# Windowed attention and a feed-forward layer: the loads of transposed probabilities of pairs 4 to 7 are issued by ACT instead of SyncE, and the first batch's order is planned anew

## Chip, core and metric

The kernel runs on one core of a Trainium2 chip. The metric is the time of one execution in microseconds (us), measured on the device. Engines are named as in the profile: PE is TensorE (matmuls), DVE is VectorE, ACT is ScalarE, POOL is GpSimd, SP is SyncE, which issues DMAs. PE accumulates in PSUM banks; the other engines but POOL read them.

## What is computed

Attention over 8 batches and 8 heads, with a window of 32 positions to each side and 32 global positions, and then a feed-forward layer with a leaky slope over all 4608 rows:

```python
k_all = concat([k_g, k_l]);  v_all = concat([v_g, v_l])
out_g = softmax(scale * q_g @ k_all.T) @ v_all            # 32 global rows of a head
s_ll  = where(abs(i - j) <= 32, scale * q_l @ k_l.T, -1e9)
s_l   = concat([scale * q_l @ k_g.T, s_ll])
out_l = softmax(s_l) @ v_all                               # 512 local rows of a head
x = concat([out_g, out_l]) as 4608 x 512
h = x @ w_in                                               # 512 x 2048
g = max(h, 0) + alpha * min(h, 0)
out = g @ w_out                                            # 2048 x 512
```

The weights arrive as float64 and are decoded on the chip into an upper and a lower float32r part.

## The kernel before

Two heads of one batch form a pair; a batch has four pairs, 32 in all. A batch of 512 rows goes through 16 blocks f of the feed-forward layer (128 hidden units each). While PE multiplies the blocks of one batch, the attention of the next batch's pairs is woven in between. The first batch is special: pairs 0 to 3 are computed ahead of it, and in it the weights are decoded, block by block, while pairs 4 to 7 are computed. From the second batch on, the decoded weights are in place.

The order of the first batch on every engine is not written by hand. `early` (L153) lists operations with an engine, a cost in us, the operations that they need and, for some, a due time; `Plan.run` (L94) is a list scheduler that picks the next operation by the earliest possible start and then by due time less a bias for its kind, and `begin` issues the instructions in the order found. Each engine then runs its own instructions strictly in that order, and waits in front of an instruction whose inputs are not there. The numbers of the plan stand in `LIST` (L38). The names of operations, as used below (a number behind a name is the pair or the block):

- S: local scores of a pair on PE; red, ex, rza, rzr, nm: its softmax on DVE, ACT and POOL, in tile p.
- G: global scores on PE; gm, gexp, gz, gsc: their softmax on DVE and ACT, in tile sg_sb.
- tq and tr: DVE transposes 32 x 32 squares of p and of sg_sb. sq and sr: four DMAs each scatter them to DRAM (scratch). hq and hr: one DMA each loads them back, fully transposed, into tile pt (512 KB and 192 KB). Pairs 0 to 3 transpose on PE instead (T, Tg).
- V: PE multiplies pt by the values (tile v); the first four matmuls need hq alone, the rest hr too. V of a pair and G of the next write one PSUM tile, and G of the next stands right behind V or one operation later. xA, xB, xg copy the result out.
- Lq, Lv, Lw: SP's loads of q and k, of v, and of raw weights; cv, ab, d1, d2, d3, ia, ca, su: decoding of half a block on ACT, DVE and POOL; wf and wo: SP's stores of decoded weights.
- f1 of a block: 12 matmuls x times w_in (rows h_ps). n, p, gh, gl: slope and split of the result (ACT, DVE, ACT, DVE). fa: 8 matmuls with gh and w_out, fb: 4 matmuls with gl (both are rows o).

There is one p, one v and one pt tile for pairs from 4 on: the next pair's red waits until sq has read p, the next Lv and hq until V is done. Every DMA of the first batch is issued by SP in the planned order. A DMA instruction that waits for its source stops SP, and all behind it. In particular hq waits on SP for the landing of sq, and hr for that of sr; the plan allowed a negative lag of 100 us between two operations of SP, that is, it did not count this wait:

```python
lag = (0.12 if e != "SP" else -100.0) if y == e else 0.3 if y == "PE" else 0.12
```

The helper lines L280 (all engines but PE) and L309 (matmuls) record every instruction, so the profile's line numbers say nothing; tiles and shapes tell the operations apart.

Of the kernel before, what the change touches and what calls it, by code (L numbers as in the profile page):

```python
# [35 lines left out]
GOFF = 1024  # L36
GROWS = {1: (0, 0), 4: (0, 1), 7: (0, 2), 10: (1, 0), 13: (1, 1), 15: (1, 2)}
LIST = dict(  # L38
    first=37.579, pace=5.504, pair0=70.66, pair=20.171, slack=2, vsub=1, ahead=4, inflight=4, near=0.1, vgl=1, half=True,
    bias=dict(tq=-6, V=12, ex=-3, ca=-3, hr=6, gz=0, xB=12, hq=-1, Lw=-7, sr=12, ab=3, gsc=0, Lq=-6, be=5, rzr=1, yh=3, gexp=-12, cv=-1, ia=1, xA=3, red=-3),  # L40
)
FAST = range(2 * NF, NB * NF)
CATCH = (16, 23, 30)
# [15 lines left out]
class Plan:  # L59
# [3 lines left out]
        self.slots = {k: [0.0] * n for k, n in slots.items()}  # L63
        self.ops, self.slack, self.near, self.bias = {}, slack, near, bias

    def op(self, name, engine, cost, needs=(), lock=False, take=(), free=(), kind=None, due=None, n=1):
        assert name not in self.ops, name
        self.ops[name] = dict(engine=engine, cost=cost, needs=[x for x in needs if x], lock=lock, take=take, free=free, kind=kind, due=due, n=n)

    def due_times(self):  # L70
        users = {n: [] for n in self.ops}
# [23 lines left out]
    def run(self):  # L95
        ops, users = self.ops, self.due_times()
        end, order = {}, []
        free = dict(PE=5.4, ACT=2.5, DVE=5.0, POOL=4.0, SP=1.2)
        lock, dma, kind = 0.0, 3.3, None
        left = {n: len(o["needs"]) for n, o in ops.items()}  # L100
        ready = {n for n, k in left.items() if k == 0}
        while ready:
            can = []
            for n in sorted(ready):
                o = ops[n]
                e = o["engine"]
# [12 lines left out]
            assert can, sorted(ready)
            t, _, n = min(can)  # L120
            e = ops[n]["engine"]
            t, _, n = min((c for c in can if ops[c[2]]["engine"] == e and c[0] <= t + self.near), key=lambda c: (c[1], c[0]))
            o = ops[n]
            cost = o["cost"]
            if e == "PE":
                cost = cost * (1.25 if t < 45 else 1.0) + (0.3 if kind != o["kind"] else 0.0)
                kind = o["kind"]
            if e == "SP":
                free[e] = t + 0.48 * o["n"]
                dma = max(dma, t + 1.6) + cost  # L130
# [22 lines left out]
def early(first, pace, pair0, pair, slack, vsub, ahead, inflight, near, vgl=0, half=False, bias={}):  # L153

    plan = Plan({"st": NST - 2, "w": NWB}, slack, near, bias)
    op = plan.op
    for P in range(9):
        pre = P < NRAW
        op(f"Lq{P}", "SP", 1.72, [f"G{P-2}", f"S{P-2}"] if P > 1 else [])
# [4 lines left out]
        due = pair0 + pair * (P - 5) if P > 4 else None  # L164
# [32 lines left out]
        last = first + pace * 15.5 if P == 8 else None  # L197
        if not pre:
            op(f"tq{P}", "DVE", 1.23, [f"nm{P}.0", f"nm{P}.1"], due=last)
            op(f"sq{P}", "SP", 1.31, [f"tq{P}"], n=4, due=last)  # L200
        if P == 8:
            break
        pb = [f"V{P-1}"] if P else []
        if pre:
            op(f"T{P}", "PE", 1.1, [f"nm{P}.0", f"nm{P}.1"] + ([f"pt0{P-1}", f"pt1{P-1}"] if P else []), kind="t", free=(("w", 1),) if P % 2 else ())
            op(f"pt0{P}", "ACT", 0.49, [f"T{P}"] + pb)
            op(f"pt1{P}", "DVE", 0.60, [f"T{P}"] + pb)
            op(f"Tg{P}", "PE", 0.45, [f"gsc{P}", f"T{P}", f"ptg{P-1}" if P else None], kind="t")
            op(f"ptg{P}", "ACT", 0.40, [f"Tg{P}"] + pb)
            lb = [f"pt0{P}", f"pt1{P}", f"ptg{P}"] + ([f"ex{P+1}.0", f"ex{P+1}.1"] if P < 3 else ["xlA1", "xlB1", "xg1"])  # L210
        else:
            op(f"tr{P}", "DVE", 0.5, [f"gsc{P}", "clear"])
            op(f"hq{P}", "SP", 1.31, [f"sq{P}"] + pb)
            op(f"sr{P}", "SP", 0.5, [f"tr{P}"], n=4)
            op(f"hr{P}", "SP", 0.5, [f"sr{P}", f"hq{P}"])
            lb = [f"hq{P}", f"hr{P}", f"mem{P+1}", f"Lq{P+1}"]
        op(f"V{P}", "PE", 2.0, [f"Lv{P}"] + lb, kind="v", free=(("w", 2),) if pre and P % 2 else ())
        if not pre:
# [7 lines left out]
        if not pre:  # L226
            c = P - NPAIR
# [8 lines left out]
    for k in range(2 * NF):  # L236
        f, j = divmod(k, 2)
# [12 lines left out]
    for t in range(NF):  # L250
        x = [f"xl{a}{P}" for P in range(NPAIR) for a in "AB"]
# [37 lines left out]
def longformer_ffn(ctx: ExitStack, tc: tile.TileContext, qk, v, w, alpha, out):  # L289
# [31 lines left out]
    sync = Engine(tc, nc.sync, pin_sync)  # L321
# [561 lines left out]
    def begin():  # L883
# [9 lines left out]
        def issue(name):  # L893
# [297 lines left out]
```

## Time and profile before

| | us |
|---|---|
| median of 3 runs | 928.39 |
| lowest to highest | 928.23 to 931.25 |
| the profiled execution, its own time | 927.88 |
| its span, first to last instruction | 926.1 |

One execution was profiled. In the table of stretches, each row has the stretch, its length, the busy time of each engine with the number of its instructions, the clock that TensorE was granted as a share of full speed, the share of the DMA engines' time that was busy, and GB/s. A row of a timeline has the start, the duration, engine, line, operation, output<-input, the number of merged instructions and, in brackets, the idle time ahead of it and what ended it. A row of waits has the engine, the tile that it was to write, whom it waited for, us in total, how often, and the longest. Rows "SPq" are SP's queue of DMA instructions.

### The profile page before, as it was taken

The page shows a single profiled execution, that of the slowest core. Times are in us where ns is not written, and L with a number is a line of the kernel's source. Part 1 is how long each engine was busy: PE and PEld are TensorE (multiplying, and loading weights), DVE is VectorE, ACT ScalarE, POOL GpSimd, SP SyncE. Part 2 cuts the span into 40 slices and gives each one's busy share as a digit, 9 for nine tenths or more (in the row PEclk, how much of TensorE's full clock was granted, in tenths as well). Part 3 has the DMA queues.
Part 4 walks back from the last instruction along what each step waited for, and adds up shares of the span by engine and source line. Part 5 has one row for each costly group of instructions (what it writes and reads, how often), then busy time and mean ns, then how long its engine had stood idle before and what let it go on. Part 6 is the DMA issues. An engine that isn't in the chain of part 4 may idle for free.

```text
span 926.1 us, 22539 instructions
## 1 busy us (share of the span) xinstructions
PE 885.9 (96%) x8668; PEld 764.9 (83%) x8668; DVE 608.7 (66%) x1676; ACT 388.6 (42%) x1166; POOL 312.7 (34%) x275
## 2 busy tenths in 40 slices
PE   7798968999999999999999999999999999999998
PEld 5676646787888888888888888888888899899898
DVE  5887757877577666866677667766686656544532
ACT  6877655553444433443345333443344322211211
POOL 3444433255444333433223323322343322222221
PEclk7889889799999999999999999999999999999999
DMA  8968977999665866586667667586657552645630
GB/s 306 348 178 322 341 252 271 337 362 358 232 208 177 294 210 197 189 277 217 211 228 253 230 224 225 187 262 217 201 181 269 185 192 91 205 160 180 205 116 24
DMA packets 86811, 211.19 MB, mean 228 GB/s; under 512 B 23985, under 2 KB 44465, under 8 KB 82865
## 3 DMA queue, kind: packets, MB, share of 16 engines
q1 hardware_dynamic: 86704, 209.76, 67.0%
q8 instruction: 68, 1.11, 0.5%
q14 instruction: 39, 0.31, 0.1%
HBM read 165.95 MB, written 43.78 MB: 226 GB/s over the span
## 4 chain that ended last, share of the span: by engine, by line
PE 67%; DMA 13%; DVE 9%; ACT 6%; SPq 2%; issue 2%; POOL 0%; DVEq 0%; ACTq 0%
PE o L309 30%; PE h_ps L309 28%; PE o_ps L309 4%; ACT p L280 3%; DMA scratch<-sg_sb 3%; PE s_ps L309 3%; DMA wraw<-in_w_dram 2%; PE g_ps L309 2%; DVE g L280 2%; DMA scratch<-p 2%; SPq L280 2%; DVE xl L280 2%; DMA pt<-scratch 1%; DMA alpha_sb<-in_alpha_dram 1%; DVE x_raw L280 1%
## 5 line engine op out<-in xcount | busy, mean ns | idle before, releaser
L280 POOL TENSOR_TENSOR gl<-g,gh 128x512 fp32r<-128x512 f32 (+1 forms) x128 | 159.1, 1243 | 375.8 <-ACT gh L280 306.0
L309 PE MATMUL h_ps<-xh,wt 128*128 128x256 f32 (+1 forms) x1120 | 241.0, 309 | 4.1 <-DVE wt L280 3.7
L309 PE MATMUL o<-gh,wo 128*128 128x512 f32 (+1 forms) x1024 | 244.3, 381 | 0.0
L280 ACT CAST gh<-g 128x512 fp32r<-128x512 f32 (+1 forms) x144 | 85.8, 596 | 306.5 <-DVE g L280 304.2
L309 PEld LDWEIGHTS o<-gh,wo 128*128 128x128 f32 x1024 | 176.8, 188 | 31.9 <-issue 0.4
L309 PEld LDWEIGHTS h_ps<-xh,wt 128*128 128x128 f32 x1120 | 182.4, 189 | 24.4 <-issue 6.1
L309 PE MATMUL h_ps<-xl,wt 128*128 128x256 f32 (+1 forms) x560 | 171.6, 306 | 0.8 <-DVE xl L280 0.8
L309 PE MATMUL o<-gl,wo 128*128 128x512 f32 (+1 forms) x512 | 131.1, 378 | 0.0
L280 DVE TENSOR_SCALAR g<-h_ps,alpha_sb 128x512 f32<-128x512 f32 (+1 forms) x128 | 91.5, 715 | 41.1 <-PE h_ps L309 35.4
L309 PEld LDWEIGHTS h_ps<-xl,wt 128*128 128x128 f32 x560 | 105.8, 189 | 6.6 <-DVE xl L280 1.0
L309 PE MATMUL h_ps<-xh,s 128*128 128x256 f32 x576 | 105.4, 279 | 2.9 <-DVE h_ps L280 2.0
L309 PEld LDWEIGHTS o<-gl,wo 128*128 128x128 f32 x512 | 92.8, 188 | 18.4
L280 POOL TENSOR_TENSOR p<-p,rz 128x512 f32<-128x512 f32 x64 | 69.2, 1101 | 101.1 <-DVE rz L280 95.2
L309 PEld LDWEIGHTS h_ps<-xh,s 128*128 128x128 f32 x576 | 90.7, 188 | 8.1 <-issue 4.0
L280 DVE TENSOR_TENSOR h_ps<-u,h_ps 128x256 f32<-128x256 f32 x144 | 61.1, 424 | 49.1 <-PE h_ps L309 47.5
L280 ACT ACTIVATE p<-p,mn 128x128 f32<-128x128 f32 x224 | 86.9, 396 | 4.8 <-DVE mn L280 4.8
L280 DVE SCALAR_TENSOR_TENSOR g<-h_ps,g 128x512 f32<-128x512 f32 (+1 forms) x128 | 84.1, 657 | 4.2
L309 PE MATMUL h_ps<-xl,s 128*128 128x256 f32 x288 | 80.6, 280 | 0.9 <-DVE xl L280 0.7
L280 DVE TENSOR_TENSOR u<-u,h_ps 128x256 f32<-128x256 f32 x96 | 40.3, 420 | 62.1 <-PE h_ps L309 38.7
L280 POOL TENSOR_TENSOR wt<-wt,wr 128x512 int32<-128x512 int32 x32 | 45.8, 1433 | 93.4 <-DVE wt L280 73.4
L309 PE MATMUL o_ps<-pt,v 128*64 128x32 f32 (+1 forms) x1600 | 59.8, 234 | 15.2 <-DMA pt<-scratch 13.2
L309 PEld LDWEIGHTS o_ps<-pt,v 128*64 128x64 f32 x1600 | 55.2, 149 | 22.4 <-DMA pt<-scratch 10.7
(88 smaller groups left out, 1046.1 us busy)
## 6 DMA issues: line engine op xcount, KB each, us to landing
wo<-wo SPq DMA_DIRECT2D x128, 512.0 KB, 4.4
v<-in_v_dram SPq DMA_DIRECT2D x30, 1024.0 KB, 5.8
qk<-in_qk_dram SPq DMA_DIRECT2D x32, 672.0 KB, 7.0
wraw<-in_w_dram SPq DMA_DIRECT2D x32, 512.0 KB, 7.4
scratch<-p SPq DMA_DIRECT2D x112, 128.0 KB, 3.0
pt<-scratch SPq DMA_DIRECT2D x28, 512.0 KB, 5.5
wo<-wt SPq DMA_DIRECT2D x16, 512.0 KB, 8.5
out_dram<-ost SPq DMA_DIRECT2D x32, 256.0 KB, 3.3
```

The source lines that it names most:

```text
L280: ins = op(*a, **k)
L309: ins = nc.tensor.matmul(*a, **k)
```

## The change

The plan may give a DMA to ACT (`move`, with the list `aq`), and `LIST` names hq and hr. On ACT such an operation costs 0.45 us in the plan, starts when what it needs has landed, and lands 2.2 us plus twice its transfer later. The lag of -100 us between two SP operations stays for all but names that begin with h. A DMA is counted 2.0 us from issue to transfer instead of 1.6, and PE's work after 45 us is counted 5% longer. The numbers in `LIST` were searched anew: among them `inflight`, which lets cv run six half blocks ahead of su instead of four, `vgl`, by which gl is split between POOL (even blocks) and DVE (odd blocks) where DVE did all, and the biases of all kinds. `scatter` and `fetch_pt` take the queue as an argument. Code behind the first batch is not changed; pairs from 8 on still load through SP.

```diff
 LIST = dict(
-    first=37.579, pace=5.504, pair0=70.66, pair=20.171, slack=2, vsub=1, ahead=4, inflight=4, near=0.1, vgl=1, half=True,
+    first=37.895, pace=5.449, pair0=70.632, pair=19.178, slack=2, vsub=1, ahead=4, inflight=6, near=0.1, vgl=2, half=True, aq="hq hr",
...
-                    lag = (0.12 if e != "SP" else -100.0) if y == e else 0.3 if y == "PE" else 0.12
+                    lag = -100.0 if y == e == "SP" and n[0] != "h" else 0.3 if y == "PE" else 0.12
...
-                cost = cost * (1.25 if t < 45 else 1.0) + (0.3 if kind != o["kind"] else 0.0)
+                cost = cost * (1.25 if t < 45 else 1.05) + (0.3 if kind != o["kind"] else 0.0)
...
-                dma = max(dma, t + 1.6) + cost
+                dma = max(dma, t + 2.0) + cost
                 stop = dma + 0.8
+            elif o["dma"]:
+                free[e] = t + cost
+                dma = max(dma, t + 2.0) + o["dma"]
+                stop = free[e] + 2.2 + 2 * o["dma"]
...
+    def move(name, dma, needs, n=1, due=None):
+        if name.rstrip("0123456789") in aq:
+            op(name, "ACT", 0.45 * n, needs, dma=dma, due=due)
+        else:
+            op(name, "SP", dma, needs, n=n, due=due)
...
-            op(f"hq{P}", "SP", 1.31, [f"sq{P}"] + pb)
-            op(f"sr{P}", "SP", 0.5, [f"tr{P}"], n=4)
-            op(f"hr{P}", "SP", 0.5, [f"sr{P}", f"hq{P}"])
+            move(f"hq{P}", 1.31, [f"sq{P}"] + pb)
+            move(f"sr{P}", 0.5, [f"tr{P}"], 4)
+            move(f"hr{P}", 0.5, [f"sr{P}", f"hq{P}"])
...
-    def fetch_pt(P, x):
+    def fetch_pt(P, x, queue=sync):
         sc = scratch.pop((P, x)).rearrange("j k c n -> (j k) (c n)")
         o, n = ((0, 1024), (GOFF, 384))[x]
-        sync.dma_start(new_pt(P)[:, o : o + n], sc)
+        queue.dma_start(new_pt(P)[:, o : o + n], sc)
...
-                {"t": transpose_dve, "s": scatter, "h": fetch_pt}[k[0]](n, "qr".index(k[1]))
+                if k[0] == "t":
+                    transpose_dve(n, "qr".index(k[1]))
+                else:
+                    {"s": scatter, "h": fetch_pt}[k[0]](n, "qr".index(k[1]), act if plan.ops[name]["engine"] == "ACT" else sync)
```

The instructions' order, engine by engine, moves in the first batch. SP's rows for pair 5 before, from wo2 over sq5, wf6, hq5, a weight load and sr5 to hr5:

```order
L280 DMA wo<-wt 128x1024
L280 DMA scratch<-p 32x4x256 x4
L280 DMA wf<-wt 128x512
L280 DMA pt<-scratch 128x1024
L280 DMA wraw<-in_w_dram 128x1024
L280 DMA scratch<-sg_sb 32x4x96 x4
L280 DMA pt<-scratch 128x384
```

SP's rows of the change from sq5 to sr5 (the helper's line is L291 now):

```order
L291 DMA scratch<-p 32x4x256 x4
L291 DMA wraw<-in_w_dram 128x1024
L291 DMA wo<-wt 128x1024
L291 DMA qk<-in_qk_dram 128x1344
L291 DMA v<-in_v_dram 128x2048
L291 DMA wf<-wt 128x512
L291 DMA wraw<-in_w_dram 128x1024
L291 DMA wo<-wt 128x1024
L291 DMA wa<-wt 128x2x256
L291 DMA wraw<-in_w_dram 128x1024
L291 DMA scratch<-sg_sb 32x4x96 x4
```

The two loads are gone from SP, nine other DMAs stand between the two scatters where three did (wf6, hq5 and one weight load), and sq5 stands ahead of one weight load, of wo2, of Lq7 and, like before, of sr5.

ACT's rows around hq5 in the change: gexp5, the load, then cv, ab, gsc5 and n5:

```order
L291 CAST gh<-g 128x512
L291 ACTIVATE wraw<-wraw 128x512
L291 CAST wt<-wt 128x512
L291 ACTIVATE sg_sb,gz<-g_ps,gm 128x3x3x32
L291 DMA pt<-scratch 128x1024
L291 ACTIVATE wr<-wraw 128x512
L291 ACTIVATE wraw<-wraw 128x512
L291 ACTIVATE sg_sb<-sg_sb,gz 128x384
L291 ACTIVATE g<-h_ps 128x512
```

Before, the same place on ACT had no DMA; gexp5 was followed by yh0 and gsc5. The load now stands in ACT's order, ahead of the weights' decoding, of gsc5 and of n5. hr5 stands further on, behind n6, ab18 and cv17 and ahead of gh6.

PE's rows ahead of V5 (its first row is o_ps<-pt,v), before:

```order
L309 MATMUL h_ps<-xh,wt 128x512 x2
L309 MATMUL h_ps<-xl,wt 128x512
L309 MATMUL h_ps<-xh,wt 128x512 x2
L309 MATMUL h_ps<-xl,wt 128x512
L309 MATMUL o_ps<-pt,v 64x32 x2
```

and in the change:

```order
L320 MATMUL h_ps<-xl,wt 128x512
L320 MATMUL o_1007<-gh,wt 128x512 x2
L320 MATMUL o_1008<-gh,wt 128x512 x2
L320 MATMUL o_1009<-gh,wt 128x512 x2
L320 MATMUL o_1010<-gh,wt 128x512 x2
L320 MATMUL o_1007<-gl,wt 128x512
L320 MATMUL o_1008<-gl,wt 128x512
L320 MATMUL o_1009<-gl,wt 128x512
L320 MATMUL o_1010<-gl,wt 128x512
L320 MATMUL o_ps<-pt,v 64x32 x2
```

fa5 and fb5 stand ahead of V5 now, behind it before. V4 has moved behind fb1 and fa2 in the same way, V6 behind fb8 and V7 behind fb11. In the names of the plan, PE's order from G5 to V7 is now: G5 fa3 f15 fb3 S6 fa4 f16 fb4 f17 fa5 fb5 V5 fa6 G6 fb6 f18 fa7 S7 fb7 f19 fa8 f110 fb8 V6 fa9 G7 fb9 f111 fa10 S8 fb10 f112 fa11 f113 fb11 V7 (f110 is f1 of block 10). Before it was: G5 fa2 f15 fb2 S6 fa3 f16 fb3 fa4 fb4 f17 V5 fa5 f18 fb5 G6 fa6 S7 fb6 f19 fa7 fb7 f110 fa8 V6 fb8 G7 fa9 f111 fb9 S8 fa10 f112 fb10 f113 fa11 V7.

More of the change, by code (lines that the diff above doesn't have):

```diff
@@ L38 @@
 LIST = dict(
-    first=37.579, pace=5.504, pair0=70.66, pair=20.171, slack=2, vsub=1, ahead=4, inflight=4, near=0.1, vgl=1, half=True,
-    bias=dict(tq=-6, V=12, ex=-3, ca=-3, hr=6, gz=0, xB=12, hq=-1, Lw=-7, sr=12, ab=3, gsc=0, Lq=-6, be=5, rzr=1, yh=3, gexp=-12, cv=-1, ia=1, xA=3, red=-3),
+    first=37.895, pace=5.449, pair0=70.632, pair=19.178, slack=2, vsub=1, ahead=4, inflight=6, near=0.1, vgl=2, half=True, aq="hq hr",
+    bias=dict(tq=-9, V=10, ca=-3, hr=6, hq=-13, Lw=17, ab=3, Lq=33, be=17, rzr=13, yh=-6, gexp=-15, xA=-3, red=-6, fb=9, p=-11, nm=12, tr=-3, ptg=1, mk=25, yl=2, n=-3, xlB=12, gh=4, T=1, al=24, fa=9, Tg=7, f=-12, wo=-3, G=12, mn=-4, rza=6, wf=-3, ex=-4, ia=1, mem=1, cv=-1, pt=-3),
 )
@@ L64, in __init__, with op @@
         self.ops, self.slack, self.near, self.bias = {}, slack, near, bias
-    def op(self, name, engine, cost, needs=(), lock=False, take=(), free=(), kind=None, due=None, n=1):
+    def op(self, name, engine, cost, needs=(), lock=False, take=(), free=(), kind=None, due=None, n=1, dma=None):
         assert name not in self.ops, name
-        self.ops[name] = dict(engine=engine, cost=cost, needs=[x for x in needs if x], lock=lock, take=take, free=free, kind=kind, due=due, n=n)
+        self.ops[name] = dict(engine=engine, cost=cost, needs=[x for x in needs if x], lock=lock, take=take, free=free, kind=kind, due=due, n=n, dma=dma)
     def due_times(self):
@@ L150, in run, with early @@
         return order
-def early(first, pace, pair0, pair, slack, vsub, ahead, inflight, near, vgl=0, half=False, bias={}):
+def early(first, pace, pair0, pair, slack, vsub, ahead, inflight, near, vgl=0, half=False, aq="sq sr hq hr", bias={}):
     plan = Plan({"st": NST - 2, "w": NWB}, slack, near, bias)
     op = plan.op
+    def move(name, dma, needs, n=1, due=None):
[3 more added lines that the diff above has]
+            op(name, "SP", dma, needs, n=n, due=due)
     for P in range(9):
@@ L199, in early @@
             op(f"tq{P}", "DVE", 1.23, [f"nm{P}.0", f"nm{P}.1"], due=last)
-            op(f"sq{P}", "SP", 1.31, [f"tq{P}"], n=4, due=last)
+            move(f"sq{P}", 1.31, [f"tq{P}"], 4, last)
         if P == 8:
@@ L616, in transpose_dve, with scatter @@
             vec.transpose(seg, seg)
-    def scatter(P, x):
+    def scatter(P, x, queue=sync):
         t, n = (ps[P], 1024) if x == 0 else (sg_sb, 384)
@@ L622, in scatter @@
             src = t[32 * c : 32 * c + 32, :].rearrange("k (j n) -> k j n", j=4)
-            sync.dma_start(scratch[P, x][:, :, c, :].rearrange("j k n -> k j n"), src)
+            queue.dma_start(scratch[P, x][:, :, c, :].rearrange("j k n -> k j n"), src)
     def transpose_q(P, x):
```

## The prediction

> **What bounds the kernel now.** I read the page first, then a table of stretches, then the waits of TensorE (PE) inside the stretch that is not full.
>
> ```profile
> PE 885.9 (96%) x8668; PEld 764.9 (83%) x8668; DVE 608.7 (66%) x1676; ACT 388.6 (42%) x1166; POOL 312.7 (34%) x275
> ...
> PE   7798968999999999999999999999999999999998
> ...
> PEclk7889889799999999999999999999999999999999
> ```
>
> PE is the bound over the whole span, but its busy tenths and its granted clock both dip in the first seven of 40 slices. That is the first batch, the only part the change orders anew. The table of stretches cuts there: the first block of the feed-forward part starts at 48.5 us, the last product of the first batch ends at 181.5.
>
> ```profile
> core 0: us, PE busy (x) PEld busy (x) DVE busy (x) ACT busy (x) POOL busy (x), PEclk, DMA share, GB/s
> 0.00:48.50 48.50, 36.66 (x666) 27.70 (x666) 35.23 (x113) 38.27 (x134) 18.77 (x31) 0.79 0.87 320
> 48.50:181.50 133.00, 114.25 (x904) 89.64 (x898) 99.31 (x279) 85.48 (x219) 47.98 (x36) 0.88 0.82 284
> 181.50:280.00 98.50, 98.32 (x955) 79.45 (x954) 69.66 (x190) 42.01 (x136) 49.38 (x45) 1.00 0.83 289
> 280.00:926.00 646.00, 636.72 (x6154) 568.07 (x6152) 404.49 (x1098) 222.80 (x678) 196.58 (x164) 1.00 0.61 200
> 100.00:120.00 20.00, 19.39 (x167) 14.84 (x163) 16.43 (x33) 14.09 (x28) 9.17 (x7) 0.92 1.01 396
> ```
>
> From 181.5 on PE is full at clock 1.00, so nothing is to be had there and whatever the first batch gives up should reach the end unchanged. Between 48.5 and 181.5 PE stands still for 133.0 - 114.25 = 18.75 us, and is granted 0.88 of its clock in the rest. What it waits for:
>
> ```profile
> PE o_ps L309 <- DMA pt<-scratch: 13.0, 5, 4.8
> PE h_ps L309 <- DVE wt L280: 3.7, 2, 2.6
> PE o_ps L309 <- DMA scratch<-sg_sb: 1.3, 1, 1.3
> ```
>
> So 14.3 of 18.75 us are the products V4 to V7 standing for the loads hq and hr (pt<-scratch). After each stop the matmuls run slowly:
>
> ```profile
> 92.92 0.66 PE L309 MATMUL h_ps<-xh,wt 128*128 128x512 f32 x1 [2.62 <-DVE wt L280]
> ...
> 128.53 0.31 PE L309 MATMUL o_ps<-pt,v 128*64 128x32 f32 x4 [3.03 <-DMA pt<-scratch]
> 133.63 2.56 PE L309 MATMUL o_ps<-pt,v 128*64 128x64 f32 x44 [4.79 <-DMA pt<-scratch]
> ...
> 137.02 2.08 PE L309 MATMUL o<-gl,wt 128*128 128x512 f32 x4
> ```
>
> The same work without a stop stands further on in the chain of work that ended last (its first line below is f10, the first block, after a stop), with one row of scores from the timeline:
>
> ```profile
> 48.63 4.62 PE h_ps L309 x12
> ...
> 185.37 2.96 PE o L309 x12
> 188.33 2.75 PE h_ps L309 x12
> 191.08 2.75 PE o L309 x12
> ...
> 196.57 1.52 PE o_ps L309 x48
> 198.10 0.94 PE g_ps L309 x20
> ...
> 207.45 1.16 PE L309 MATMUL s_ps<-qk 64*32 64x128 f32 x64
> ```
>
> At full clock the stretch would be 16 f1 at 2.75 (44.0), 14 pairs of fa and fb at 2.75 together (38.5), four times V with the G behind it (1.52 + 0.94) and S (1.16), 14.5, and 0.2 us for each of eight changes of kind (2.96 after a score instead of 2.75), 1.6: **98.6 us**. PE was busy for 114.25, so slow clock costs 15.65 us. f10 alone takes 4.62 us, 1.9 over; the other 13.75 us go with 18.75 us of stops, **0.73 us for each us stopped**.
>
> **The change, part by part.** *The loads leave SyncE (SP).* From the waits of SP and of ACT in the stretch, and SP's timeline in pair 6:
>
> ```profile
> SPq L280 <- DMA scratch<-p: 14.2, 6, 4.6
> ...
> SPq L280 <- DMA scratch<-sg_sb: 9.5, 4, 4.0
> ...
> ACT wr L280 <- DMA wraw<-in_w_dram: 22.8, 11, 6.2
> ...
> 115.92 3.26 SPq L280 DMA_DIRECT2D scratch<-p  x4
> 123.92 0.34 SPq L280 DMA_DIRECT2D pt<-scratch  x1
> ...
> 124.84 1.96 SPq L280 DMA_DIRECT2D scratch<-sg_sb  x4
> 131.09 0.34 SPq L280 DMA_DIRECT2D pt<-scratch  x1
> ```
>
> In pair 6 the scatter sq6 is issued by 119.2, hq6 at 123.92: SP stood for its landing, and everything behind it stood too, weight loads and sr6 with it. Over the batch that is 14.2 + 9.5 = 23.7 us of a stopped queue; ACT's 22.8 us of waiting for raw weights are in part its echo. In the new order SP goes on with weights, v, qk and stores while a scatter lands. The sr6 scatter could have gone out at once.
>
> *What is late next.* V6 needs hr6, whose chain begins at G6. A PE row, a DVE row and the stretch's DMA issues (count, size of one, median us to landing) price it:
>
> ```profile
> 108.33 0.70 PE L309 MATMUL g_ps<-qk 128*64 128x288 f32 x6
> 118.30 0.57 DVE L280 STREAM_TRANSPOSE sg_sb<-sg_sb 128x384 f32<-128x384 f32 x1
> ...
> scratch<-p SPq DMA_DIRECT2D x20, 128.0 KB, 6.2
> pt<-scratch SPq DMA_DIRECT2D x4, 512.0 KB, 4.2
> ...
> scratch<-sg_sb SPq DMA_DIRECT2D x20, 48.0 KB, 4.3
> pt<-scratch SPq DMA_DIRECT2D x4, 192.0 KB, 2.6
> ```
>
> G6 ends at 109.03 and its transposed tile is ready at 118.87: 9.8 us through DVE and ACT. The scatter takes 1.4 us to reach its fourth issue and 4.3 to land, the load 2.6: 18.1 us from G6 to V6. In the new order PE has between them three f1 (8.25), two fa (3.7), three fb (2.75) and S7 (1.1), 15.8 us, so V6 still waits 2.3. V7 has the same work between, 2.3 again. V5 has one fa more, 17.7 us, 0.4 left. V4's chain starts far earlier and leaves nothing. The move of V5 behind fa5 and fb5 is what covers it, that of V6 and V7 behind fb8 and fb11 gives 0.9 each; all are in the counts. **V waits: 14.3 become 5.0.** If sr lands as late as the larger p scatters (6.2 instead of 4.3) they are 10.7; if as soon as the small load (2.6), 1.2.
>
> *Weights.* 3.7 us of stops for wt: the loads are no longer held, but PE asks sooner. Between nothing and all of it I take 2.5, and 0.5 for the two small stops of 0.4 us outside the rows above: **8.0 us stopped in all**.
>
> *ACT takes eight issues and their waits.* An issue is 0.34 us in the rows above; under a full queue SP has rows such as this:
>
> ```profile
> 99.68 1.52 SPq L280 DMA_DIRECT2D wraw<-in_w_dram  x1
> ```
>
> So eight cost 2.7 to 12 us of ACT; I take 3, the unblocked rows being of the same kind. With 85.5 busy that makes 88.5 of about 114 us, off the bound. Behind a stopped ACT stand the raw weights' first steps, n and gh, and for them PE. No row has an ACT DMA wait: it lies between nothing, if the scatter has landed when ACT arrives (in the new rows weight work stands ahead of the load), and 23.7 us, all that SP had; near the lower end I put 1.5 us on PE.
>
> *gl of even blocks to GpSimd (POOL), odd on DVE.* The two forms:
>
> ```profile
> L280 POOL TENSOR_TENSOR gl<-g,gh 128x512 fp32r<-128x512 f32 (+1 forms) x128 | 159.1, 1243 | 375.8 <-ACT gh L280 306.0
> 83.14 0.68 DVE L280 TENSOR_TENSOR gl<-g,gh 128x512 fp32r<-128x512 f32 x1
> ```
>
> Eight times: DVE loses 5.4 us of 99.3, POOL gains 9.9 on 48.0 (to 58 of 114). fb comes 0.56 us later at the earliest; in both orders a whole fa (1.8 us) runs between gh and fb, and hides it. Without that cover it is 8 x 0.56 = 4.5 us.
>
> *Inflight 6, biases, lags and the 2.0 us of DMA lead* are only numbers that set the order; they issue nothing themselves. Before 48.5 us the order changes as well (G0 ahead of S0); PE stands there for 48.50 - 36.66 = 11.8 us, so it can give more than it takes, and I take nothing.
>
> *DMA.* 37.8 MB move in this stretch (284 GB/s by 133 us). At the 396 GB/s of the 100 to 120 stretch that is 95 us, so 114 us leaves room of a sixth, though landings get later.
>
> **Sum.** 98.6 + 1.9 (f10) + 8.0 stopped + 5.8 slow clock behind it (8.0 x 0.73) = 114.3; with 1.5 for ACT 115.8 against 133.0: 17.2 us less. The profiled execution took 927.88 us (span 926.1 and 1.8 around it), half a us under the median of 928.39. 927.9 - 17.2 = **910.7 us**.
>
> The Trainium skill, "DMA: Bandwidth & Descriptors", section "Issuing engines are not separate DMA queues", speaks against this: DMAs from any engine run on the same 16 DMA engines, and another issuing engine saves only the sequencer's issue time. By that rule the gain is the first rival below; the trace agrees that issue time is small (0.34 us), but also shows that here it is the wait in SP's order that costs, of which the rule says nothing.
>
> **Rivals.**
> 1. *The load moves, the wait does not matter*: hr's chain and the DMA backlog set V as before, and only SP's eight issues are saved, 8 x 0.34 = 2.7 us: 925.2. For it: V6 has both sq6 and sr6 late. Against it: sr6's tile was ready at 118.87 and issued at 124.84, six us of pure queue.
> 2. *Half of it*: DMA lag adds up from pair to pair because landings lie closer (scatter 6.2, V waits 10.7, wt 3.7, ACT 3): 14.8 stopped with 10.8 slow, 98.6 + 1.9 + 25.6 + 3 = 129.1 would save 4; between that and the forecast, 917 to 924.
> 3. *Nothing is left*: no stops at all, 98.6 + 1.9 = 100.5, 32.5 less, 895; with V waits of 1.2 and nothing else, 102.6, 897. Against it: the chain from G to hr is longer than PE's work between.
> 4. *ACT becomes the stopped queue, and it is slower.* At hq ACT waits for the scatter; n, gh and cv stand behind it. From f11 to fa1 PE has f12, fb0 and f13, 6.4 us; n, p and gh take some 1.9 (0.6 for each, as the 596 ns of a gh cast on the page), so a stop of up to 4.5 us is absorbed and one beyond reaches PE, say like the 2.62 us before f17, with 2.62 x 0.73 = 1.9 slow behind. If each of eight stops did so, 8 x 4.5 = 36 us come, against 14.3 x 1.73 = 24.7 that go: 11 slower, 939. It decides where scatters land over 4.5 us after ACT arrives; SP's longest such wait was 4.6, so it needs ACT to arrive as early as SP did, each time.
>
> ```profile
> L280 ACT CAST gh<-g 128x512 fp32r<-128x512 f32 (+1 forms) x144 | 85.8, 596 | 306.5 <-DVE g L280 304.2
> ```
>
> **How the numbers follow.** The forecast, 904 to 917 (5 us of stops in all and nothing for ACT, to 11 us and 3 for ACT), gets 0.62; rival 2 gets 0.17; rival 3, under 904, 0.08; rival 1, within 0.3% (2.8 us, about what a measurement of this kernel can tell from no change), 0.05; slower by rival 4 0.08. So faster 0.87, same 0.05, slower 0.08. The range leaves out rivals 1 and 4 and most of the lower tail: 902 to 923.
>
> **What would show it.** Right: no DMA wait of some us on SP for scratch; V5 to V7 with stops of 0 to 3 us; the last fb of the batch near 164 us instead of 181.5; the stretch after it still full at clock 1.00. Rival 4: ACT idle before its pt loads, 5 us each, and PE waiting for gh or wt. Rival 2: weights landing later and more ACT time on wraw. Wrong altogether: new stops behind the first batch, where the next loads of pair 8 or of weights meet a later backlog.

## The result, and the profile after

| | before, us | after, us |
|---|---|---|
| median of 12 runs each, on one chip | 929.40 | 921.39 |
| lowest to highest | 924.5 to 935.3 | 916.3 to 926.8 |
| the profiled execution (span) | 927.88 (926.1) | 926.75 (925.0) |

The ratio is 0.9912, with a 95% interval of 0.9887 to 0.9938: 8.2 us faster (5.8 to 10.5), where 17.2 were forecast. The profiled execution of after was the slowest of its twelve; a second one, of the same kernel, is the first run below (920.4 us).

The stretches of after, cut where its fb13 ends (columns as in the prediction's table of stretches):

```profile
0.00:48.50 48.50, 31.70 (x611) 23.68 (x620) 34.13 (x109) 38.12 (x136) 19.27 (x31) 0.96 0.87 317
48.50:175.00 126.50, 114.64 (x959) 91.54 (x959) 103.02 (x277) 85.51 (x219) 56.77 (x44) 0.88 0.88 303
175.00:280.00 105.00, 104.17 (x981) 84.21 (x980) 70.90 (x207) 46.81 (x155) 50.14 (x46) 1.00 0.78 274
```

fb13 ends at 175.0 us (second row of PE's timeline here), 6.5 sooner than before; f10 (first row) starts 1.5 us later than the 48.56 of before. The prediction calls 181.5 us the end of the batch's last product. It is the end of fb13, the 14th of 16; fb14 and fb15 follow without a stop and end at 193.8 us before and at 187.3 after, 6.5 sooner too. The prediction's sum counts 14 pairs of fa and fb, so it fits the stretch as cut. Below, "the batch ends" means the end of fb13 in every run.

```profile
50.08 1.22 PE L320 MATMUL h_ps<-xh,wt 128*128 128x512 f32 x2
...
173.93 1.08 PE L320 MATMUL o<-gl,wt 128*128 128x512 f32 x4
```

PE's waits in the batch have one large entry left, the loads of transposed probabilities; those for wt are gone. The timeline shows the stops of V5, V6 and V7 in front of the matmuls that need hr (V4 has the other 1.9 us):

```profile
PE o_ps L320 <- DMA pt<-scratch: 11.9, 4, 3.9
```

```profile
104.61 1.65 PE L320 MATMUL o_ps<-pt,v 128*64 128x64 f32 x26 [3.67 <-DMA pt<-scratch]
...
132.06 2.14 PE L320 MATMUL o_ps<-pt,v 128*64 128x64 f32 x36 [3.92 <-DMA pt<-scratch]
...
157.92 2.29 PE L320 MATMUL o_ps<-pt,v 128*64 128x64 f32 x38 [2.40 <-DMA pt<-scratch]
```

SP does what the change says. Its longest waits in the stretch are now for PE and DVE, not for landings of scratch (14.2 and 9.5 us before):

```profile
SPq L291 <- PE g_ps L320: 20.0, 7, 7.9
SPq L291 <- DVE p L291: 13.2, 3, 8.0
SPq L291 <- PE s_ps L320: 7.6, 1, 7.6
SPq L291 <- DVE sg_sb L291: 7.3, 4, 5.5
```

But the DMA issues of the batch (count, size, median us to landing) land later. On ACT's queue hr takes 5.4 us instead of 2.6 and hq 8.5 instead of 4.2; sr, still on SP, takes 6.3 instead of 4.3:

```profile
pt<-scratch ACTq DMA_DIRECT2D x4, 512.0 KB, 8.5
...
scratch<-sg_sb SPq DMA_DIRECT2D x16, 48.0 KB, 6.3
pt<-scratch ACTq DMA_DIRECT2D x4, 192.0 KB, 5.4
```

Before, SP issued nothing more while it stood for sr, and hr met idle DMA engines: the DMA view of before from 100 to 136 us, in 40 slices of 0.9 us, falls to under 75 GB/s around 123 and under 50 around 131 us, where hq6 and hr6 were issued:

```profile
GB/s 355 403 374 338 319 360 396 432 437 432 378 396 421 405 389 440 411 422 401 399 402 393 381 165 73 40 0 50 223 323 332 332 144 16 0 48 339 415 371 279
```

Now SP issues weights in that time. That was the first theory after the result (theory A): the gain was halved because hr and sr land behind SP's bulk.

### The profile page after: what moved, and what is told of

It reads as the page before. It is cut to its first block, busy times and chain, and to the rows that moved or that the text cites. A ratio compares the mean times of both kernels' runs of the same rounds, so it can differ in the third digit from the quotient of the medians.

```text
span 925.0 us, 22508 instructions
## 1 busy us (share of the span) xinstructions
PE 885.7 (96%) x8667; PEld 766.5 (83%) x8668; DVE 608.5 (66%) x1668; ACT 387.8 (42%) x1166; POOL 321.5 (35%) x283
## 4 chain that ended last, share of the span: by engine, by line
PE 72%; DMA 11%; DVE 9%; ACT 6%; issue 1%; SPq 1%; POOL 0%; ACTq 0%; DVEq 0%
PE o L320 32%; PE h_ps L320 28%; PE o_ps L320 5%; PE s_ps L320 4%; PE g_ps L320 3%; DMA scratch<-sg_sb 3%; ACT p L291 3%; DVE g L291 3%; DMA pt<-scratch 3%; DMA wraw<-in_w_dram 2%; DMA qk<-in_qk_dram 2%; DVE xl L291 2%; DVE x_raw L291 1%; SPq L291 1%; DVE wsum L291 1%
## 5 line engine op out<-in xcount | busy, mean ns | idle before, releaser
L291 POOL TENSOR_TENSOR gl<-g,gh 128x512 fp32r<-128x512 f32 (+1 forms) x136 | 170.0, 1250 | 391.6 <-ACT gh L291 315.9
L291 ACT CAST gh<-g 128x512 fp32r<-128x512 f32 (+1 forms) x144 | 85.9, 596 | 315.5 <-DVE g L291 308.8
L320 PEld LDWEIGHTS o<-gh,wo 128*128 128x128 f32 x1024 | 177.6, 188 | 32.4 <-issue 0.4
L291 DVE TENSOR_SCALAR g<-h_ps,alpha_sb 128x512 f32<-128x512 f32 (+1 forms) x128 | 91.6, 716 | 43.3 <-PE h_ps L320 37.6
L291 POOL TENSOR_TENSOR p<-p,rz 128x512 f32<-128x512 f32 x64 | 70.5, 1117 | 107.7 <-DVE rz L291 101.0
L291 DVE TENSOR_TENSOR h_ps<-u,h_ps 128x256 f32<-128x256 f32 x144 | 61.1, 424 | 51.4 <-PE h_ps L320 49.8
L291 ACT ACTIVATE p<-p,mn 128x128 f32<-128x128 f32 x224 | 86.8, 395 | 4.2 <-DVE mn L291 4.0
L291 DVE SCALAR_TENSOR_TENSOR g<-h_ps,g 128x512 f32<-128x512 f32 (+1 forms) x128 | 84.2, 658 | 4.3
L291 DVE TENSOR_TENSOR u<-u,h_ps 128x256 f32<-128x256 f32 x96 | 40.3, 420 | 65.0 <-PE h_ps L320 42.1
L291 POOL TENSOR_TENSOR wt<-wt,wr 128x512 int32<-128x512 int32 x32 | 42.9, 1342 | 62.9 <-DVE wt L291 46.3
```

Of the source, the lines that this page charges most:

```text
L291: ins = op(*a, **k)
L320: ins = nc.tensor.matmul(*a, **k)
```

## Experiments

Each kernel was timed beside the kernel before on one chip, and its ratio is to that; not all ran on the same chip, so ratios compare better than medians. "Changed kernel" is after; the "new order" is the order of its plan. A list of MOVED names an operation and, with it, the one that it now stands behind.

**after_again**: no edit.

> The changed kernel once more, so that the other runs of this chip have it beside them. Every theory: 916 to 927 us, 5 to 10 under the kernel before; PE stops for the pt loads at V4 to V7 of 10 to 14 us in all; the loads hr land 5 to 6 us and hq 8 to 9 us from their issue on ACT's queue.

919.36 us, ratio 0.9884 [0.9858, 0.9910]. Stops for pt 11.4 us, hr lands in 5.0 to 6.4 us. Its batch ends at 170.2 us, five sooner than in the first profile.

**warm_first**: the warm-up ahead of G0.

```diff
             elif k == "G":
+                if n == 0:
+                    score_banks(0, WARM)
                 global_scores(n)
```

> The changed kernel, with the eight warm-up matmuls of S0 put back ahead of G0 (in the change G0 stands first and waits 4.85 us for the first q and k, and the warm-up runs behind it). Theory 'the start lost 2.3 us to this': the warm-up runs from 1.5 us on, S0 ends near 8 us instead of 14, f10 starts at 48 to 49 us instead of 50.8, and the time is 1.5 to 4 us under that of the changed kernel. Rival, the start is set by something else (decoding of weights, softmax of pair 3): f10 stays at 50 to 51 us and the time is the same within 1 us.

917.37, [0.9834, 0.9888]. f10 moves from 48.9 to 47.0 us, yet the intervals overlap, and on another base (sp_warm below) the same edit gave 913.4 against 913.6. Without the edit f10 starts 0.4 us later than before in the profile of after_again and 1.7 in that of loads_on_sp; that this costs as much at the end isn't shown.

**sr_first**: SP issues sr5 to sr7 ahead of bulk that stood in front of them.

```diff
+BEHIND = [("Lw17", "sr5"), ("wo3", "sr5"), ("wf6", "sr5"), ("Lw23", "sr6"), ("Lw24", "sr6"), ("wf9", "sr6"), ("wo6", "sr6"), ("Lw30", "sr7"), ("wf12", "sr7"), ("wo9", "sr7")]
```

> The changed kernel, with bulk DMAs on SP moved from just ahead of the small scatters sr5, sr6, sr7 to just behind them (three, four and three DMAs of 256 to 512 KB). Theory A, SP no longer held by waits now runs ahead with bulk, and the small scatters stand behind it (for a free place among the eight DMAs under way, and in the transfers): sr issue to landing falls from 8.9, 8.6 and 8.4 us to 4 to 6, hr of pairs 5 to 7 lands 2 to 4 us sooner, PE's stops at V5 to V7 fall from 10.0 us to 1 to 4, and the time falls by 6 to 12 us. Rival B, it is ACT's queue that is slow: hr still takes 5 us or more from issue, sr gains at most 1 us, stops stay at 8 to 12, the time is the same within 2 us. Rival C, the weights now come late: new stops for wt eat what is won.

927.27, [0.9950, 0.9993]: slower than the changed kernel by 6 to 8 us. The scatters did land sooner (5.9, 3.0 and 4.5 us from issue), so SP's backlog is real. But hr did not leave. ACT's timeline shows a cv that stood for its raw weights, just delayed on SP, and hr behind it in ACT's order, though sr5 had landed at 92.4:

```profile
97.55 0.66 ACT L292 ACTIVATE wr<-wraw 128x512 int32<-128x512 uint32 x1 [4.20 <-DMA wraw<-in_w_dram]
97.71 0.33 ACTq L292 DMA_DIRECT2D pt<-scratch  x1
```

PE's stops for pt rose to 17.3 us. A load on a computing engine waits for all that stands ahead of it there.

**filled**: matmuls on idle data in PE's stops.

```diff
+FILL = {4: 8, 5: 16, 6: 16, 7: 10}
...
+                keep_warm(outs[n][0], FILL.get(n, 0))
                 pv_all(n, *outs[n])
```

> The changed kernel, with 8, 16, 16 and 10 matmuls on idle data ahead of V4, V5, V6 and V7, into the bank that V then overwrites: the stops are filled with work that nobody needs, as long as the stops were. Theory 'each stop over some 1.5 us costs about 3.3 us of slow clock behind it': the granted clock stays at 0.97 or more from 60 to 175 us (0.87 in the changed kernel), the blocks behind V run at 2.75 us and the time falls by 6 to 11 us. Rival, the slow clock has another cause (load on the chip, the kind of matmul): the clock stays near 0.87, the time is the same or up to 3 us longer where a fill is longer than its stop.

918.77, [0.9856, 0.9914]: no different from after_again, although the granted clock rose (after_again, then filled):

```profile
48.50:170.00 121.50, 109.62 (x930) 86.49 (x913) 100.84 (x275) 84.91 (x217) 56.16 (x43) 0.93 0.90 314
```

```profile
48.50:170.00 121.50, 117.31 (x1013) 93.79 (x1009) 103.11 (x277) 86.03 (x219) 57.48 (x44) 0.97 0.91 317
```

The 50 matmuls at 0.23 us (f1's 2.75 by 12) fill 11.5 us, and 3.9 us of stops for pt are left: together more than the 11.4 that the stops had. Faster work between the stops mainly brings PE to V earlier, where it waits for the same hr. In the one profile of each, f10 to fb13 takes 118.8 us here and 121.3 in after_again, so a small part may be won. Most of the slow clock isn't a term of its own here.

**loads_on_sp**: the change without its title.

```diff
-{"s": scatter, "h": fetch_pt}[k[0]](n, "qr".index(k[1]), act if plan.ops[name]["engine"] == "ACT" else sync)
+{"s": scatter, "h": fetch_pt}[k[0]](n, "qr".index(k[1]), sync)
```

> The changed kernel's order on every engine, but hq and hr of pairs 4 to 7 issued by SP, at the same place between the others: the change without its title. Theory 'the gain comes from SP no longer standing for landings': SP stands again for sq and sr (15 to 25 us in all), bulk loads come late, and the time goes back to 926 to 932 us. Rival 'the gain comes from the new order, in which V4 to V7 stand behind more of PE's work': 918 to 922 us, hr lands 2.5 to 3.5 us from issue, since SP issues nothing while it waits, and PE's stops at V stay under 12 us.

913.59, [0.9793, 0.9861]: **faster than the changed kernel**, and by its ratio the largest gain of all runs. It is the rival, and more of it than the rival said: stops for pt are 7.8 us, of which 1.9 are V8's, behind the batch, and hr lands in a median of 3.9. The scatters of sr5 to sr7 land as late as with the loads on ACT (10.1, 7.5 and 8.2 us from the first issue, 9.2, 5.8 and 8.4 in after_again): with either queue sr is late, and only hr lands sooner here. SP's waits for sr came back, but only 4.1 us of them. PE's and SP's waits and the issues of hr:

```profile
PE o_ps L320 <- DMA pt<-scratch: 7.8, 4, 3.0
```

```profile
SPq L291 <- DMA scratch<-sg_sb: 4.1, 3, 2.2
```

```profile
pt<-scratch SPq DMA_DIRECT2D x4, 192.0 KB, 3.9
```

**old_order_act**: the title alone, in the kernel before.

```diff
-{"t": transpose_dve, "s": scatter, "h": fetch_pt}[k[0]](n, "qr".index(k[1]))
+{"t": transpose_dve, "s": scatter, "h": fetch_pt}[k[0]](n, "qr".index(k[1]), *([act] if k[0] == "h" else []))
```

> The order of before on every engine, but hq and hr of pairs 4 to 7 issued by ACT at the places where SP had them in the plan: the title of the change alone. Theory 'SP no longer held is the gain': some 5 to 9 us under the kernel before (920 to 925), sr goes out as soon as its tile is there, hr lands 5 us from issue. Rival 'the order is the gain': within 3 us of before. Second rival, ACT is the stopped queue: in this order hq stands ahead of weight work and of n and gh with nothing to cover its wait, ACT idles 2 to 4 us at each load, and the time is 930 us or more.

930.06, [0.9974, 1.0019]: no change. PE's waits and ACT's say why (the profiled execution took 934.81 us, the longest of its twelve). The stops for pt nearly vanish, 13.0 to 2.4 us, as the prediction had it, and stops for wt grow from 3.7 to 14.3, since ACT stands 6.6 us in front of hr and 4.6 in front of hq with weight work and gh behind:

```profile
PE h_ps L309 <- DVE wt L280: 9.9, 3, 5.2
PE h_ps L309 <- ACT wt L280: 4.4, 2, 4.0
...
PE o_ps L309 <- DMA pt<-scratch: 2.4, 3, 1.3
```

```profile
ACT wt L280 <- DMA scratch<-sg_sb: 6.6, 1, 6.6
...
ACT gh L280 <- DMA scratch<-p: 4.6, 1, 4.6
```

So it is the new order that gains, and the queue that costs: with the old order 930 on either queue, with the new one 913.6 on SP and 919.4 on ACT.

**sr_ahead**: only stores behind the scatters, and hr ahead of the cv on ACT.

```diff
+MOVED = {... "sr5": "tr5", "wf6": "sr5", "wo3": "wf6", "hr5": "p6", ... "sr6": "tr6", "wo6": "sr6", "wf9": "wo6", "cv24": "hr6", ... "wo9": "sr7", "wf12": "wo9", ... "hr7": "rza8.0"}
```

> The changed kernel; on SP the stores wf and wo that stand just ahead of sr5, sr6, sr7 are moved behind them (two, two and two; the weight loads stay ahead), and on ACT hr5, hr6 and hr7 stand ahead of the cv that precedes them, so that they don't wait for its raw weights. Theory A, backlog on SP makes the scatters late and the ACT order then the load: sr lands 1.5 to 4 us sooner, hr is issued as soon, PE's stops at V5 to V7 fall from 7 to 10 us to 3 to 6, and the time is 3 to 6 us under the changed kernel's 919 to 921. Rival, the pace is the whole loop from one V over G and its softmax to the next V, of which the landing is a part that has other work beside it: 1 to 3 us less. Rival, ACT stops at hr ahead of cv and PE then waits for wt or gh: no gain or slower.

915.68, [0.9812, 0.9885]: 3.7 us under after_again, with overlapping intervals. sr lands 6.0, 5.4 and 7.0 us from issue instead of 9.2, 5.8 and 8.4, and stops for pt fall to 9.5 only.

**g_early_hand**: G of the next pair, with its softmax and scatter, ahead of V.

```diff
+MOVED = {"hr4": "red5.0", "G5": "cv14", "gm5": "cv13", "gexp5": "sq5", "gz5": "xA4", "gsc5": "d114", "tr5": "Lw15", "sr5": "cv16", "hr5": "wf6", "G6": "tq6", ... "sr6": "tr6", ... "hr6": "xg5", "G7": "ab23", ... "sr7": "tr7", ... "hr7": "wo9"}
```

> The changed kernel; the global scores G5, G6, G7 no longer stand behind the V of the pair before but ahead of it on PE (they share a PSUM tile with it, in other columns), and their softmax, transpose, scatter and hr move up with them on DVE, ACT and SP: 8 to 15 us sooner. Theory R, the batch is paced by the loop V4, G5, softmax, tr5, sr5, hr5, V5, G6 and so on (27 us for each turn, of which PE's own work is some 24 at full clock): with the loop cut no V waits for hr any more, stops for pt loads fall from 11 us to 0 to 3 us (V4 may keep its own), the clock stays at 0.95 or more, and the time is 8 to 14 us under the changed kernel: 906 to 912. Rival, PE's wait only moves to the weights (DVE is busy for 83% of the stretch): new stops for wt or g, 915 to 920. Rival, the earlier work stands in front of the decoding on DVE and ACT and delays it: no gain.

924.53, [0.9926, 0.9977]. Half of theory R holds: the V stops are gone altogether, so they did hang on the loop from V to the next V. In their place ACT stood 5.8 us at hr5, with n and gh behind it, and PE 6.8 us at the next f1; then weights:

```profile
90.48 0.66 ACT L292 ACTIVATE wr<-wraw 128x512 int32<-128x512 uint32 x1 [5.82 <-DMA scratch<-sg_sb]
```

```profile
PE h_ps L321 <- DVE g L292: 6.8, 1, 6.8
PE o L321 <- ACT gh L292: 3.9, 4, 2.2
PE o L321 <- ACT wt L292: 2.7, 1, 2.7
```

**g_early_sp**: nearly the same on the base of loads_on_sp (hr5 behind "d313", hr6 behind "gl7", hr7 behind "ia23"; hr4 stays, and gz6 and some loads and stores have other places).

> The new order with all loads on SP (913.6 us), and G5, G6, G7 with their softmax, transpose and scatter ahead of V4, V5, V6, as in the run that cut the loop with the loads on ACT (924.5, V without a stop, but ACT stood 5.8 us at hr5 with n, gh and cv behind it). On SP hr stands a few DMAs behind hq, and ACT issues nothing. Theory R, the loop paced the batch and ACT's stop ate the gain: PE's stops at V4 to V7 under 3 us in all, no stop of ACT for scratch, 905 to 911. Rival, the decoding of weights and the split of g on ACT and DVE bound the batch next: stops for wt, g or gh of 4 us or more, 911 to 916.

928.11, [0.9948, 0.9993]: the rival, and worse than it said. V waits only 0.2 us for pt, and PE's stops are for gh, g and wt (the three longest rows); ACT waits 23.3 us for raw weights, where it waited 15.1 in loads_on_sp. With the loop cut by hand, the split of g and the decoding seem to pace the batch; the two were not separated.

```profile
PE o L321 <- ACT gh L292: 5.7, 2, 5.5
PE h_ps L321 <- DVE g L292: 4.1, 1, 4.1
PE o L321 <- ACT wt L292: 3.4, 1, 3.4
```

**tq_late**: loads_on_sp, with tq6, tq7 and their sq and hq at their old places.

```diff
+MOVED = {"tq6": "ia19", "sq6": "p8", "hq6": "sq6", "tq7": "ia26", "sq7": "n11", "hq7": "sq7"}
```

> The new order with the loads on SP (913.6 us), but the transposes tq6 and tq7 and with them sq6, hq6, sq7, hq7 moved back to where the order of before had them: tq just ahead of tr on DVE, sq and hq just ahead of sr on SP (in the new order the tile p is out 14 to 18 us sooner, 98.7 instead of 115.9 us for pair 6). Theory T, the old order lost its time because SP stood with a late p in front of sr, so that hr6 and hr7 came late: hq6 is issued near 121 us instead of 106, hr6 lands 4 to 8 us later, PE's stops grow by 5 to 10 us and the time by 6 to 12: 919 to 926. Rival, other parts of the order (gl on POOL, decoding six half blocks ahead, the place of V) bring the gain: 912 to 917.

927.56, [0.9959, 1.0005]: moving six operations takes back 14 of the 16 to 17 us. SP's timeline is the old picture: the scatter of p at 117.55, hq6 behind its landing, sr6 behind that though its tile was there, and hr6 last; stops for pt are 18.3 us.

```profile
117.55 1.77 SPq L292 DMA_DIRECT2D scratch<-p  x4
123.02 0.34 SPq L292 DMA_DIRECT2D pt<-scratch  x1
123.45 1.81 SPq L292 DMA_DIRECT2D scratch<-sg_sb  x4
...
128.28 0.78 SPq L292 DMA_DIRECT2D pt<-scratch  x1
```

**before_tq_early**: the converse, in the kernel before.

```diff
+MOVED = {"rzr6.1": "rza6.1", "p7": "rzr6.1", "d318": "p7", "nm6.0": "xB5", "nm6.1": "nm6.0", "tq6": "ia18", "sq6": "d120", "hq6": "ab22", "nm7.0": "gh10", "nm7.1": "nm7.0", "tq7": "ia24", "sq7": "tq7", "Lv7": "sq7", "Lw28": "Lv7", "hq7": "Lw28", "wo8": "hq7"}
```

> The kernel before, loads on SP, with one thing of the new order: the last steps of the local softmax of pairs 6 and 7 (rzr, nm, tq) and their scatter sq stand earlier on DVE, POOL and SP, sq6 behind wo5 and sq7 behind wf10's group, with hq6 and hq7 close behind. Theory T, a late p held SP and with it sr and hr: tq6 ends near 106 us instead of 116, tq7 near 136 instead of 147, sr6 goes out as its tile is ready, hr6 lands at 126 to 129 instead of 133.6, hr7 at 157 to 159 instead of 162, and the time falls by 5 to 10 us to 920 to 925. Rival, it takes the whole of the new order: 927 or more.

928.24, [0.9958, 0.9998]. hr6 lands at 129.8 instead of 133.6, hr7 at 157.3 instead of 162.1, and stops for pt halve, but PE's stops for wt grow from 3.7 to 5.9 us:

```profile
PE o_ps L310 <- DMA pt<-scratch: 6.7, 4, 2.9
PE h_ps L310 <- DVE wt L281: 5.9, 2, 3.8
```

Even so the batch ends 3.9 us sooner in this profile (177.6), and that is lost behind it: what follows takes 750.3 us instead of 744.6. The early tail is needed but not enough; the new order has it together with a decoding that keeps ahead (no stop for wt). Which part of the plan does the latter was not separated, but gl is not it:

**gl_dve**: loads_on_sp, with gl of even blocks back on DVE.

```diff
-lower_g(n, g[n], SL, pool if plan.ops[name]["engine"] == "POOL" else vec)
+lower_g(n, g[n], SL, vec)
```

> The new order with the loads on SP (913.6 us), but gl of the even blocks back on DVE, at the same place in the order. The prediction put the move to POOL at nothing. If that holds: 912 to 916, DVE busy about 5 us more in the stretch. Rival, DVE's place in the loop (global softmax, transposes, decoding) is short of time: 918 or more, with stops of PE for wt or g.

913.50, [0.9808, 0.9861], the same as loads_on_sp.

**hr_on_sp** and **hq_on_sp**: the changed kernel with one of the two loads on ACT, hq in the first (shown), hr in the second.

```diff
-{"s": scatter, "h": fetch_pt}[k[0]](n, "qr".index(k[1]), act if plan.ops[name]["engine"] == "ACT" else sync)
+{"s": scatter, "h": fetch_pt}[k[0]](n, "qr".index(k[1]), act if k == "hq" else sync)
```

> The changed kernel with hr alone back on SP; hq stays on ACT. Theory H, the 6 us that ACT's issuing costs come from hr's landing: on ACT's queue it shares the DMA engines with the bulk loads that SP goes on issuing (5 to 6.4 us from issue), while SP waiting for sr has nothing more to issue and hr lands in 3.2 to 4.4: 912 to 916, hr 3 to 4.5 us. Rival, it is the wait on ACT ahead of hq (n, gh, cv behind it): 918 to 922 as with both on ACT.

> The changed kernel with hq back on SP; hr stays on ACT. With both on ACT it is 919.4, with hr alone on SP 918.2, with both on SP 913.6. If the large load on ACT's queue is what costs: 912 to 916. If each of the two on ACT costs the same by itself: 917 to 920, hr landing 5 us or more from issue.

918.19, [0.9846, 0.9897], and 919.55, [0.9853, 0.9911]. By these medians either load on ACT costs about what both do; hr took 5.6, 5.0 and 3.4 us in the first, 5.1, 6.5 and 5.1 in the second.

**sp_warm**, **sp_sr_ahead** and **sp_best**: repairs on the base of loads_on_sp (the warm-up, the stores behind sr, and both).

> Two repairs together: the new order with all loads on SP, and the warm-up matmuls ahead of G0. If they add (16 us and 2 us under before): 911 to 913, f10 at 47 to 49 us, the last fb of the batch at 163 to 165. If the warm-up's gain goes into longer stops for the loads: 913 to 915.

> The new order with all loads on SP (913.6 us), and the stores wf and wo that stand just ahead of sr5, sr6 and sr7 moved behind them on SP; with the loads on ACT the same move (and hr ahead of a cv) gave 915.7 against 919.4. If the bytes ahead of sr set when it lands: sr5 to sr7 land 1 to 3 us sooner and the time is 910 to 912. If the loop has other limits by now: 913 to 915.

> All repairs together: the new order, all loads on SP, stores behind the small scatters, warm-up matmuls ahead of G0. 908 to 912 if they add; 913 to 914 if stops take what is won, as the warm-up alone showed on this base (913.4).

913.44, [0.9805, 0.9863]; 915.24, [0.9816, 0.9869]; 915.15, [0.9796, 0.9870]: none beats loads_on_sp. In sp_warm the batch ends 3.9 us sooner than in loads_on_sp (162.2 against 166.2), but what follows takes 748.9 us instead of 745.4. In sp_sr_ahead hr gives back what sr wins (hr6 5.6 us instead of 4.4): the stores now stand beside it.

## Why the prediction was wrong

**Where the bound lies: right, but "unchanged" was not.** All that changed lies in the first batch and before it, and from 175 to 280 us PE is busy for 104.17 of 105.00 us at clock 1.00. But what followed the batch took 744.6 us in the profile of before and some 745 to 751 in those of the new order. In the profile of after, 5.4 of the 6.5 us won were lost again by the end; in that of loads_on_sp 0.8 of 15.4. Small new stops behind the batch, a sign that the prediction named, are part of it: V8 and V9 wait for pt 0.8 us in after, 1.8 in after_again and 2.5 in loads_on_sp, against 0.2 before. The rest of the loss isn't explained.

**The step that failed is the cause**, "the loads leave SyncE": the 23.7 us of SP's standing were taken as what the change frees. They were freed, and the title alone gave nothing (930.06 against 930.77). The prediction's rival 4 is what happened there: ACT became the stopped queue, as far as the gain went. I had put its price "near the lower end", 1.5 us, because weight work stands ahead of the load in the new rows. In the new order the price is 5 to 6 us (919.4 against 913.6).

**The order was undersized.** It got "0.9 each" for the places of V6 and V7. It is worth 16 to 17 us, nearly the forecast sum by another way; that loads_on_sp falls into the forecast range is luck. Its decisive part was not in the prediction at all. The rows for SP shown in front of it stop at pair 5; in pair 6 tq6, and so sq6, is 16 us earlier (DVE's timeline of before, then of after), out long before sr6 has its tile:

```profile
114.57 1.28 DVE L280 STREAM_TRANSPOSE p<-p 128x512 f32<-128x512 f32 x2
```

```profile
98.61 1.29 DVE L291 STREAM_TRANSPOSE p<-p 128x512 f32<-128x512 f32 x2
```

SP's waits of before had it as their first row, which the prediction left out:

```profile
SPq L280 <- DVE p L280: 17.4, 5, 7.7
```

That row alone proves nothing, since SP waits 11.6 us for p in loads_on_sp too; tq_late does, where a late p in pairs 6 and 7 brings the old time nearly back. I read SP's wait for sq's landing as the fault of the queue; in pairs 6 and 7 it was the fault of a late p.

**What is late next: the sum was near, its parts were not.** For V6 (rows of PE and DVE, the second from DVE's tile view: one transpose of 567 ns at 117.4):

```profile
111.03 0.70 PE L320 MATMUL g_ps<-qk 128*64 128x288 f32 x6
```

```profile
L291 DVE STREAM_TRANSPOSE sg_sb<-sg_sb x1: 567/567/567, 117.4 to 117.4; 128x384 f32<-128x384 f32 x1
```

From G6 to the tile it took 6.2 us (forecast 9.8), sr 8.6 to landing (5.7 with its issues), hr 5.3 (2.6): 20.3 with the steps between, instead of 18.1. PE worked 16.4 us in between, forecast 15.8, and V6 waited 3.92 instead of 2.3. V7 waited 2.40 (2.3), V5 3.67 (0.4), V4 1.86 (nothing): 11.9 us instead of 5.0. The term that was mis-sized is the landing of sr and hr; durations were taken from a trace in which SP's stops kept the DMA engines free at just that time. Rival 2 had named this lag, and its 917 to 924 is where the median fell.

**Slow clock: 5.8 us forecast, 13.5 in the profile** (four times some 3.4, below) and 8.5 in that of after_again. Yet filled shows that most of it isn't to be added: V starts when hr lands, and slow work only shortens the stop in front of it.

**Weights and gl: near.** Stops for wt went from 3.7 to nothing (2.5 forecast), and gl on POOL is worth nothing either way.

**The start: not nothing.** f10 comes 1.5 us later in the profile of after and 0.4 in that of after_again; with the warm-up matmuls ahead of G0, which waits for the first load, it comes 1.6 us sooner than before (warm_first).

The Trainium skill, "DMA: Bandwidth & Descriptors", section "Issuing engines are not separate DMA queues", says that another issuing engine saves no more than the sequencer's issue time. I weighed it with a chance of 0.05. The runs agree with it in the old order: 930.06 against 930.77 us. In the new one ACT as issuer is 5 to 6 us worse, of which the rule says nothing.

**Open.** Why even one of the two loads on ACT costs the whole 5 to 6 us. Against loads_on_sp the landings of hr5 to hr7 are longer by 6.0 us together in after_again and by 5.6 in hq_on_sp, which would be about all of it, but by 2.9 only in hr_on_sp, which is as slow. What of the new order keeps the decoding ahead wasn't tried either.

## What to carry to other kernels

When a change moves work to another queue and replans the order at once, price the two apart: run, or at least read, the new order with the old queue. When a queue stands for a landing, ask first why that transfer was issued so late; its producer may be the fault, and then another queue only moves the wait to an engine with work behind it. And a stop in front of a transfer that closes a loop is not won back by faster work between: here PE came to it sooner and waited for the same transfer.

## What the runs showed that was not expected

**Eight DMAs under way.** The program hands eight semaphores in turn to the DMAs of SP and ACT together, and in the trace of after the DMAs were issued as the one eight before them landed (us, from the trace's issue and landing times):

```
DMA           issued   landed   the DMA eight before, landed
sr5, second   92.67    99.04    v 92.65
sr5, third    93.36    99.21    wf 93.35
sr5, fourth   95.49    99.37    wraw 95.48
wraw          98.65   104.14    wraw 98.63
```

A small scatter so waits for bulk twice, to be issued and to land.

**The clock's price for a stop comes in steps.** Windows of after, in tens of us, and then of after_again, the same kernel (only stretch, length, busy times, clock, DMA share and GB/s are of use):

```profile
70.00:80.00 10.00, 8.14 (x83) 6.78 (x83) 8.77 (x24) 9.04 (x25) 7.04 (x6) 0.80 0.73 260
80.00:90.00 10.00, 10.00 (x100) 7.33 (x99) 7.56 (x17) 5.67 (x11) 3.79 (x4) 0.86 0.99 327
100.00:110.00 10.00, 6.33 (x73) 5.31 (x72) 6.20 (x13) 7.88 (x16) 3.92 (x3) 0.67 0.98 352
...
130.00:140.00 10.00, 7.94 (x78) 6.71 (x79) 7.24 (x18) 5.67 (x11) 4.61 (x4) 0.66 0.87 260
...
150.00:160.00 10.00, 7.60 (x66) 6.26 (x66) 7.67 (x19) 8.60 (x25) 6.23 (x6) 0.90 0.80 283
160.00:170.00 10.00, 10.00 (x59) 7.84 (x58) 8.51 (x19) 3.62 (x7) 2.56 (x2) 0.76 0.71 209
```

```profile
70.00:80.00 10.00, 7.43 (x84) 5.50 (x83) 8.09 (x19) 8.82 (x23) 7.04 (x6) 0.83 0.71 245
...
100.00:110.00 10.00, 6.28 (x67) 5.59 (x68) 6.01 (x12) 7.47 (x15) 3.06 (x3) 0.70 0.94 327
110.00:120.00 10.00, 10.00 (x104) 7.41 (x104) 8.30 (x26) 5.42 (x13) 3.62 (x3) 0.96 0.97 360
...
130.00:140.00 10.00, 9.94 (x91) 8.13 (x92) 6.26 (x18) 6.48 (x14) 3.90 (x3) 0.83 0.99 334
...
150.00:160.00 10.00, 8.00 (x83) 6.50 (x81) 7.23 (x14) 8.63 (x22) 4.64 (x5) 0.83 0.64 204
```

In after the stops of 1.86, 3.67, 3.92 and 2.40 us cost (2.0 + 1.4), 3.3, 3.4 and (1.0 + 2.4) us of clock: 3.3 to 3.4 each. In after_again those of 2.57, 4.57, 2.25 and 2.00 us cost 1.7, (3.0 + 0.4), 1.7 and 1.7. So the price follows neither the length of a stop nor a fixed rate. Windows cut to fit show a granted clock of 0.50 from 76.03 to 82.86 us in after and from 76.67 to 80.08 in after_again: around these eight stops the clock is halved for 6.83 or for 3.41 us, which makes 3.4 or 1.7 us. In sr_ahead the stops of 1.95 and 1.89 us that end at 101.79 and 107.69 us cost nothing (clock 1.00 from 95 to 115). What decides between nothing, 1.7 and 3.4 us wasn't tested. The prediction's 0.73 us for each us stopped, a mean over the stops of before, fits after_again (8.5 for 11.4) and not after (13.5 for 11.9).

The Trainium skill, "TensorE: Matmul & The Clock Gate", section "HAM oscillation — how this bites in real kernels", warns of idle gaps of PE above some 3.4 us. Here the measurement decides: in after 1.86 us of standing still were enough.
